# Scores and V of eight attention heads as eight float32 products in 64 x 32 tiles, with V taken from the float32 W1 in every batch

## Chip, cores and metric

One core of one Trainium2 chip. The metric is the device time of one execution in microseconds (us). TensorE (PE) does the matrix products, VectorE (DVE), ScalarE (ACT) and GpSimd (POOL) the elementwise work, SyncE (SP) issues the DMAs.

## What is computed

Inputs are float64. Attention between 512 positions and 32 state rows per head, 8 batches of 8 heads with 64 columns each, then two MLPs over 4608 rows:

```python
scores = scale * np.matmul(x, state.transpose(0, 1, 3, 2))   # x [8, 8, 512, 64], state [8, 8, 32, 64]
a = softmax(scores)
xread = np.matmul(a, state)
a2 = softmax(scale * np.matmul(state, x.transpose(0, 1, 3, 2)))
sread = np.matmul(a2, x)
x = rows of concatenate([xread, sread], axis=2)              # 4608 x 512
h = x @ w_in                                                 # 512 x 1024
solu = h * softmax(h); ln = layer_norm(solu) * g_ln
y = ln @ w_out                                               # 1024 x 512
y = y @ moe2_w_in; out = (y * sigmoid(1.702 * y)) @ moe2_w_out   # 2048 wide
```

`softmax` divides by the sum plus 1e-9. The kernel uses that xread @ w_in = a @ (state @ w_in): V = state @ w_in has only 32 rows per head.

## The kernel before

The program is written as steps (engine, cost, function, tiles read and written, a due time `key`) that `Plan.plan` (line 170) puts in an order per engine by a list schedule: among the steps that are ready it takes the one that its costs let start first, PE steps by key, others by due time. Constants such as `KF`, `LOOK`, `M2A`, `COLD` and `PAIR` steer it. SBUF tiles are slots of kinds ("s" 71 slots of 2 KB a partition, "t", "y", "d"), PSUM is eight banks of 128 x 512 float32 (`banks`, line 157). Products of full precision are three fp32r products of high and low parts (`mm3`, line 430, lines 431 to 433: hi x hi, lo x hi, hi x lo). `to_f32` (line 440) makes float32 of a float64 tile with two ACT, three DVE and one POOL instruction (line 460), `split` (line 463) the high and low part (line 467).

`attention(b)` (line 513) handles one batch. A tile `xT[j]` holds two heads, 2j and 2j+1, on 64 partitions each. The states of the heads stand in `S2`, two fixed tiles with zeros in the other head's half, so that `state_T` (line 557) gives a block-diagonal `stT`, two transposes of 128 x 128 per batch. `scores(g)` (line 574, products at line 580) multiplies it with `xT` for four heads: two products of 128 rows (half of them zeros) by 64 columns of the array and 512 moving columns in float32, one in each column half. Two such groups make a batch; the softmax over positions and over states follows, `e2_T` (line 624) transposes, `read_s` (line 635, products at line 642) makes sread as 32 small products of 128 rows by 32 columns.

V has two forms. Batches 0 and 1 use `state_w1` (line 673, products at line 680): four groups like the scores' per batch, with the float32 W1 tiles as moving operand, high part by ACT (line 684), low part by DVE (line 685) straight from PSUM. From batch `DIRECT = 2` on, `state_w1_both` (line 688) takes two batches at once: stT is split, W1 is split into `W1s` (line 1230), and eight `mm3` triples make V of two batches in halves that ACT copies to SBUF (line 720) and `split` cuts. In odd batches ("turned") the heads stand the other way round.

`mlp1` (line 755) multiplies the softmax A with V and does SoLU and layer norm, `z_T` (line 830) transposes, `mlp1_out` (line 849) multiplies with W2. The second MLP (`up`, line 1007, `down`, line 1097) is a seven-product scheme over 2 x 2 blocks, whose weights `prepare_up` (line 903) and `prepare_down` make and store in DRAM, and `load_up` (line 914) fetches once the first MLP's last product has run.

Of the kernel before, what the change touches and what calls it, by code (L numbers as in the profile page):

```python
# [25 lines left out]
KF = 11.222  # L26
LOOK = 27.436
KR = 1.553
DIRECT = 2
W1S = 20.477  # L30
ATT = -0.491
# [3 lines left out]
RK = 6  # L35
# [47 lines left out]
class Plan:  # L83
# [73 lines left out]
    def banks(self, kind, n):  # L157


        b = self.bank  # L160
        assert n == 1
        if kind == "w":
            if self.wide == 3:
# [3 lines left out]
        best = [(b[j] + (PAIR if b[j ^ 1] is not None else 0.0), b[j], (j,)) for j in range(8) if b[j] is not None]  # L167
        return min(best)[1:] if best else None
# [156 lines left out]
WAIT = 19.511  # L325
# [3 lines left out]
M1S = 14.290  # L329
M2A = 47.371  # L330
M2S = 3.016
A1 = 8.286
# [3 lines left out]
LD = 1.964  # L336
LA = 0.010
LOAD = dict(dve=LD, act=LA)
COLD = 16.0
IDLE = 2.2  # L340
XRAW = 1
BUS = 350e3

BUS0 = 180e3
BUS0T = 10.0
PAIR = 13.326
HOLDM = 1.958
HOLDW = 9.657
# [4 lines left out]
def attention_solu_gelu(ctx: ExitStack, tc: tile.TileContext, x, state, w1, w2, g_ln, w3, w4, out):  # L353
# [18 lines left out]
    SLOT = 40.411  # L372
# [14 lines left out]
    pl.kind("t", slot_p, 4)  # L387
# [36 lines left out]
    S2t = [pl.fixed(t, f"S2_{i}") for i, t in enumerate(S2)]  # L424
# [57 lines left out]
    A, V, xn, stT, W1s = {}, {}, {}, {}, {}  # L482
# [21 lines left out]
    def load_state(b):  # L504
        src = state[b].rearrange("(g h) n d -> h n g d", h=HG)

        def go(e):
            for hl in range(HG):
                e.dma_start(out=S2[b % 2][NS * hl:NS * hl + NS, :, hl % 2, :], in_=src[hl])

        do([(STQ, 3.)] if b == 0 else DMA(2.), go, writes=[S2t[b % 2]], nbytes=P * 512)

    def attention(b):
        base = (b - 1) * SLOT + (A1 if b == 1 else ATT)
        n_step = [0]
        steps = [16]

        def key():
            n_step[0] += 1
            return base + (n_step[0] - 1) * SLOT / steps[0]  # L520

        both = b >= DIRECT
        turned = both and b % 2
        xt = {}
        load_x(b, 0)
        if not turned:
            load_state(b)
# [29 lines left out]
        def state_T(c):  # L557
            p = tl("m", [P, 512], F32, f"pst{c}")
            s2 = S2t[c % 2]
            st = stT[c] = tl("t", [P, G, P], F32, f"stT{c}")  # L560

            def go(e):
                for g in range(G):
                    e.transpose(p()[:, g * P:(g + 1) * P], s2()[:, g].rearrange("p a d -> p (a d)"), ident)

            def v():
                return p()[:, 0:G * P].rearrange("p (g n) -> p g n", g=G)

            do(PE(.22), go, [s2], [p], key())
            do([("act", .27), ("dve", .33)], lambda e: copy(e, st(), v()), [p], [st])  # L570
# [3 lines left out]
        def scores(g):  # L574
            p = tl("m", [P, 512], F32, f"psc{b}_{g}")

            def go(e):
                for i in range(2):
                    jj = i ^ turned
                    e.matmul(p()[64 * i:64 * i + 64, :], stT[b]()[:, g, 64 * jj:64 * jj + 64], xt[2 * g + jj](),  # L580
                             start=True, stop=True)

            do(PE(.9), go, [stT[b], xt[2 * g], xt[2 * g + 1]], [p], key())
# [51 lines left out]
        def read_s():  # L635
            p = tl("m", [P, 512], F32, f"psr{b}")

            def go(e):
                for g in range(G):
                    for c in range(C):  # L640
                        for hl in range(HG):
                            e.matmul(p()[NS * hl:NS * hl + NS, g * D:(g + 1) * D],
                                     e2k[g]()[:, c, NS * hl:NS * hl + NS],
                                     xn[b, 2 * g + (hl // 2 ^ turned)]()[:, c, hl % 2, :],
                                     start=(c == 0), stop=(c == C - 1))

            do(PE(1.55), go, [e2k[0], e2k[1]] + [xn[b, j] for j in range(NP)], [p], key())
            sr = tl("t", [P, G, 2, D], F32, f"sr{b}")
            for g in range(G):
                do(DVE(.26), lambda e, g=g: e.tensor_scalar(  # L650
                    sr()[:, g], p()[:, g * D:(g + 1) * D].unsqueeze(1).to_broadcast([P, 2, D]),
                    r2[g]()[:, 1:2], None, op0=ALU.mult), [p, r2[g]], [sr])
            p2 = tl("m", [P, 512], F32, f"psrT{b}")

            def go2(e):
                for g in range(G):
                    e.transpose(p2()[:, g * P:(g + 1) * P], sr()[:, g].rearrange("p a d -> p (a d)"), ident)

            do(PE(.22), go2, [sr], [p2], key())
            for q in range(2):  # L660
                for a in range(2):
                    def go3(e, q=q, a=a):
                        pv = p2()[:, 0:G * P].rearrange("p (j a n) -> p j a n", a=2, n=NS)
                        o = xs[q]()[64 * a:64 * a + 64, :, b * NS:(b + 1) * NS]
                        if turned:
                            for j in range(2):
                                copy(e, o[:, j], pv[64 * a:64 * a + 64, 2 * q + 1 - j, a, :])
                        else:
                            copy(e, o, pv[64 * a:64 * a + 64, 2 * q:2 * q + 2, a, :])
                    c = 1 + bool(turned)  # L670
                    do([("act", .11 * c), ("dve", .13 * c)], go3, [p2], [xs[q]])

        def state_w1(g, f):
            p = tl("m", [P, 512], F32, f"pv{b}_{g}_{f}")
            hi = tl("s", [P, 512], F32R, f"vhi{b}_{g}_{f}")
            lo = tl("s", [P, 512], F32R, f"vlo{b}_{g}_{f}")

            def go(e):
                for jj in range(2):
                    e.matmul(p()[64 * jj:64 * jj + 64, :], stT[b]()[:, g, 64 * jj:64 * jj + 64],  # L680
                             W1[2 * g + jj, f](), start=True, stop=True)

            do(PE(.9), go, [stT[b], W1[2 * g, f], W1[2 * g + 1, f]], [p], key())
            do(ACT(.48), lambda e: e.copy(hi(), p()), [p], [hi])
            do(DVE(.6), lambda e: e.tensor_tensor(lo(), p(), hi(), op=ALU.subtract), [p, hi], [lo])
            V[b, g, f] = (hi, lo)

        def state_w1_both():


            hi = tl("s", [P, G, 4, 64], F32R, f"sthi{b}")
            lo = tl("s", [P, G, 4, 64], F32R, f"stlo{b}")
            for i in range(2):
                st = stT[b + i]

                def part(t, i=i):
                    return t()[:, :, 1:3, :] if i else t()[:, :, 0:4:3, :]

                def src(st=st):
                    return st().rearrange("p g (j n) -> p g j n", j=2)  # L700

                do([("act", .29), ("dve", .2)], lambda e, part=part, src=src: copy(e, part(hi), src()), [st], [hi])
                do([("pool", .68), ("dve", .33)], lambda e, part=part, src=src: e.tensor_tensor(
                    part(lo), src(), part(hi), op=ALU.subtract), [st, hi], [lo])
            for f in range(2):
                for g in range(G):
                    v = [tl("s", [P, 512], F32, f"v{b + i}_{g}_{f}") for i in range(2)]
                    for jj in range(2):
                        p = tl("m", [P, 512], F32, f"pv{b}_{g}_{f}_{jj}")

                        def go(e, p=p, g=g, f=f, jj=jj):
                            wh, wl = W1s[2 * g + jj, f]
                            at = [t()[:, g, 2 * jj:2 * jj + 2, :].rearrange("p i n -> p (i n)") for t in (hi, lo)]
                            mm3(p(), *at, wh(), wl(), True, True)

                        do(PE(.65), go, [hi, lo, *W1s[2 * g + jj, f]], [p], key())
                        for side in range(2):
                            t = v[side ^ jj]
                            r = slice(64 * side, 64 * side + 64)
                            do([("act", .48), ("dve", .6)], lambda e, t=t, p=p, r=r: copy(e, t()[r, :], p()[r, :]),  # L720
                               [p], [t])
                    for i in range(2):
                        V[b + i, g, f] = split(v[i], f"v{b + i}_{g}_{f}", None)
# [3 lines left out]
        if not turned:  # L727
            state_T(b)
        e0 = scores(0)
        x_T(2)  # L730
        x_T(3)
        e2_T(0, e0)
        e1 = scores(1)
        n_step[0] += 1
        if both and not turned:
# [583 lines left out]
```

## Time and profile before

| | |
|---|---|
| runs | 1121.33, 1122.02, 1122.55 us; median 1122.02 |
| profiled execution | span 1120.6 us from first to last instruction; no other time of it is given |
| busy, share of the span | PE 96%, DVE 72%, ACT 57%, POOL 26% |
| chain that ended last | PE 80%, DVE 6%, POOL 3%, ACT 3%, DMA issue 3% |
| PE clock by 40 slices | full in all but the first (9 tenths) and second (7 tenths) |

The span counts from the first instruction to the last; the runs are measured around it. A busy PE is not PE at its peak, since products are pipelined: the distance from one start to the next tells more than a duration. A float32 product shows as two records (passes), an fp32r product as one. A line can be a helper's (467, 472), then the tile tells what it is.

### The profile page before, as it was taken

Reading aid. Unit: us, or ns where it says so; the run is one execution under the profiler, and the core shown is the slowest. Engines: PE = TensorE matmul, PEld = TensorE weight load, DVE = VectorE, ACT = ScalarE, POOL = GpSimd, SP = SyncE. Lnnn points to the kernel's source line nnn. Section 1 sums busy time; section 2 is a strip of 40 time slices with the busy share of each in tenths; the row PEclk is TensorE's granted clock in tenths of the full one; section 3 lists DMA queues with packets and bytes.
Section 4 is the critical chain, followed back from the end, with each engine's and each line's share of the span. In section 5 each row is a group of like instructions: output and inputs, shape, how many; then the busy total and the mean of one; then the engine's idle time right before and its main releaser. Section 6 shows DMA issues by size and latency. Waiting matters only on the chain.

```text
span 1120.6 us, 21706 instructions
## 1 busy us (share of the span) xinstructions
PE 1080.8 (96%) x8055; PEld 977.5 (87%) x8055; DVE 802.0 (72%) x1372; ACT 639.9 (57%) x1172; POOL 286.6 (26%) x243
## 2 busy tenths in 40 slices
PE   5799999899889999999999999999999999999998
PEld 3367777677667889999999999999999999999998
DVE  7889768787887736638766755534398888788874
ACT  6588756866857547547656665545244444344341
POOL 3976653863756601401000000000000000000000
PEclk9799999999999999999999999999999999999999
DMA  8214243568663469999666757469944254344421
GB/s 238 72 58 104 69 94 97 173 135 199 178 148 94 151 158 369 343 344 314 233 236 230 245 192 261 170 224 398 389 127 131 66 171 143 105 141 151 139 88 58
DMA packets 233082, 202.78 MB, mean 181 GB/s; under 512 B 128784, under 2 KB 174864, under 8 KB 232976
## 3 DMA queue, kind: packets, MB, share of 16 engines
q1 hardware_dynamic: 232880, 201.26, 57.3%
q8 instruction: 63, 1.03, 0.4%
q14 instruction: 43, 0.35, 0.1%
q10 hardware_dynamic: 96, 0.13, 0.0%
HBM read 113.25 MB, written 82.84 MB: 175 GB/s over the span
## 4 chain that ended last, share of the span: by engine, by line
PE 80%; DVE 6%; POOL 3%; ACT 3%; SPq 3%; issue 3%; DMA 2%; DVEq 0%; POOLq 0%; ACTq 0%
PE psum L1107 9%; PE psum L1108 9%; PE psum L1109 9%; PE psum L1019 9%; PE psum L1020 9%; PE psum L1021 9%; PE psum L431 6%; PE psum L432 6%; PE psum L433 6%; SPq L815 2%; DVE sml L780 1%; PE psum L836 1%; DVE u L784 1%; DVE z L825 1%; POOL w_w L460 1%
## 5 line engine op out<-in xcount | busy, mean ns | idle before, releaser
L1107 PE MATMUL psum<-w4r,hi_g 128*128 128x256 f32 x896 | 251.7, 281 | 1.6 <-DVE oc L1118 1.6
L1109 PE MATMUL psum<-w4r,lo_g 128*128 128x256 f32 x896 | 251.5, 281 | 0.0
L1108 PE MATMUL psum<-w4r,hi_g 128*128 128x256 f32 x896 | 251.5, 281 | 0.0
L1107 PEld LDWEIGHTS psum<-w4r,hi_g 128*128 128x128 f32 x896 | 169.0, 189 | 1.8 <-ACT hi_g L472 1.8
L1109 PEld LDWEIGHTS psum<-w4r,lo_g 128*128 128x128 f32 x896 | 168.9, 189 | 0.0
L1108 PEld LDWEIGHTS psum<-w4r,hi_g 128*128 128x128 f32 x896 | 168.9, 188 | 0.0
L472 ACT CAST hi_g<-a_g 128x512 fp32r<-128x512 f32 x124 | 75.5, 621 | 128.1 <-DVE a_g L889 89.4
L460 POOL TENSOR_TENSOR w_w<-w_w,raw_w 128x512 uint32<-128x512 uint32 x48 | 66.5, 1390 | 270.0 <-DVE w_w L458 160.1
L431 PE MATMUL psum<-zhi,hi_w 128*128 128x512 f32 (+1 forms) x288 | 114.6, 398 | 6.0 <-DVE u L784 4.7
L1031 DVE TENSOR_TENSOR c<-psum,u 128x512 f32<-128x512 f32 x64 | 44.2, 690 | 93.2 <-PE psum L1021 63.9
L433 PE MATMUL psum<-zhi,lo_w 128*128 128x512 f32 (+1 forms) x288 | 110.4, 383 | 0.4 <-POOL lo_w L467 0.4
L966 DVE TENSOR_TENSOR lo_g<-a_g,hi_g 128x512 fp32r<-128x512 f32 x128 | 84.1, 687 | 20.6 <-PE psum L1108 7.4
L1003 ACT ACTIVATE t<-c 128x512 f32<-128x512 f32 x96 | 60.3, 632 | 40.6 <-DVE c L1031 40.5
L966 DVE TENSOR_TENSOR lo_g<-gr,hi_g 128x512 fp32r<-128x512 f32 x104 | 71.2, 687 | 11.9 <-ACT hi_g L472 9.2
L432 PE MATMUL psum<-zlo,hi_w 128*128 128x512 f32 (+1 forms) x208 | 78.6, 378 | 0.0
L472 ACT CAST hi_g<-gr 128x512 fp32r<-128x512 f32 x104 | 61.9, 619 | 28.8 <-PE psum L1108 15.3
L431 PEld LDWEIGHTS psum<-zhi,hi_w 128*128 128x128 f32 x288 | 54.6, 190 | 19.8 <-DVE u L784 6.4
L433 PEld LDWEIGHTS psum<-zhi,lo_w 128*128 128x128 f32 x288 | 54.5, 189 | 12.2 <-POOL lo_w L467 0.8
L1019 PE MATMUL psum<-hi_x,w3r_2h 128*128 128x256 f32 x224 | 63.0, 281 | 0.5 <-ACT x L1026 0.5
L1020 PE MATMUL psum<-lo_x,w3r_3h 128*128 128x256 f32 x224 | 63.0, 281 | 0.0
L1020 PE MATMUL psum<-lo_x,w3r_0h 128*128 128x256 f32 x224 | 63.0, 281 | 0.0
L1019 PE MATMUL psum<-hi_x,w3r_3h 128*128 128x256 f32 x224 | 62.9, 281 | 0.0
(252 smaller groups left out, 3109.2 us busy)
## 6 DMA issues: line engine op xcount, KB each, us to landing
g<-t SPq DMA_DIRECT2D x136, 256.0 KB, 3.4
gr<-g SPq DMA_DIRECT2D x136, 256.0 KB, 3.7
w4r<-w4k SPq DMA_DIRECT2D x56, 256.0 KB, 5.2
raw_w<-in_moe_w_in SPq DMA_DIRECT2D x24, 512.0 KB, 5.3
raw_w<-in_moe_w_out SPq DMA_DIRECT2D x24, 512.0 KB, 4.7
xb<-scr SPq DMA_DIRECT2D x34, 256.0 KB, 5.4
scr<-x SPq DMA_DIRECT2D x16, 512.0 KB, 3.9
out<-oc SPq DMA_DIRECT2D x32, 256.0 KB, 3.2
```

Source lines behind the costliest of these rows:

```text
L431: nc.tensor.matmul(o, lhi, rhi, start=first, stop=False)
L432: nc.tensor.matmul(o, lhi, rlo, start=False, stop=False)
L433: nc.tensor.matmul(o, llo, rhi, start=False, stop=last)
L460: do(POOL(1.23), lambda e: e.tensor_tensor(u(), u(), raw()[:, :, 0], op=ALU.add), [w, raw], [w], key=due)
L472: e.copy(o, i)
L966: do(DVE(.68), lambda e: e.tensor_tensor(flat_(lo), flat_(t), flat_(hi), op=ALU.subtract), [t, hi], [lo], key=due)
L1019: nc.tensor.matmul(o, wh()[:, k, cut], hi()[:, k, :], start=first and not mi + k, stop=False, **OPEN)
L1020: nc.tensor.matmul(o, wh()[:, k, cut], lo()[:, k, :], start=False, stop=False, **OPEN)
L1021: nc.tensor.matmul(o, wl()[:, k, cut], hi()[:, k, :], start=False, stop=bool(mi and k), **OPEN)
L1107: nc.tensor.matmul(o, hi()[:, mi, cut], wt[:, 0], start=first, stop=False, **OPEN)
L1108: nc.tensor.matmul(o, hi()[:, mi, cut], wt[:, 1], start=False, stop=False, **OPEN)
L1109: nc.tensor.matmul(o, lo()[:, mi, cut], wt[:, 0], start=False, stop=2 * j + mi == NM - 1 and u == 1, **OPEN)
```

## The change

The heads are grouped by parity: r = 0 the even heads, r = 1 the odd ones. `state_T` makes one transpose per batch, without zeros: partitions 64r to 64r+63 hold the heads of parity r, columns 32c to 32c+31 head 2c+r. A new function `by_heads` multiplies all eight heads in one step, each as a float32 product of 64 rows by 32 columns of the array, parity 0 into one PSUM bank and parity 1 into another. It serves the scores (one step per batch in place of two) and V (two steps per batch, every batch, in place of both old forms):

```diff
+        def by_heads(p, rhs):
 
             def go(e):
-                for g in range(G):
...
+                for c in range(HG):
+                    for r in range(2):
+                        e.matmul(p[r]()[NS * c:NS * c + NS, :], stT[b]()[D * r:D * r + D, NS * c:NS * c + NS],
+                                 rhs[c]()[D * r:D * r + D, :], start=True, stop=True)
+
+            do(PE(HEADS), go, [stT[b], *rhs], p, key())
...
+        def state_w1(f):
+            p = [tl("m", [P, 512], F32, f"pv{b}_{r}_{f}") for r in range(2)]
+            by_heads(p, [W1[c, f] for c in range(HG)])
+            for r in range(2):
...
+                do(ACT(.48), lambda e, hi=hi, r=r: e.copy(hi(), p[r]()), [p[r]], [hi])
+                do(DVE(.6), lambda e, hi=hi, lo=lo, r=r: e.tensor_tensor(lo(), p[r](), hi(), op=ALU.subtract),
+                   [p[r], hi], [lo])
+                V[b, r, f] = (hi, lo)
...
-        if not turned:
-            state_T(b)
-        e0 = scores(0)
+        state_T()
         x_T(2)
         x_T(3)
...
+        p = [tl("m", [P, 512], F32, f"psc{b}_{r}") for r in range(2)]
+        by_heads(p, [xt[c] for c in range(HG)])
+        e2 = [soft(r, p[r]) for r in range(2)]
...
-        if b + 1 == DIRECT:
+        if b + 1 < B:
+            attention(b + 1)
+        if b + 1 == B:
             for f in range(2):
                 for k in range(KD):
-                    W1s[k, f] = split(W1[k, f], f"w1s_{k}_{f}", b * SLOT + W1S + 2 * (k + KD * f))
-        if b + 1 < B:
-            attention(b + 1)
+                    W1s[k, f] = split(W1[k, f], f"w1s_{k}_{f}", b * SLOT - 10 + k + KD * f)
```

`soft` is the old softmax without the product. `S2`, its two memsets, `turned` and `state_w1_both` are gone; the split W1 is used for the 256 state rows' `mlp1` alone, and W1 in float32 stays until the last V. The state output needs one transpose in place of two. `banks` can give two banks at once, "t" has 8 slots in place of 4, `RK` (buffers kept free for `load_up`) is 8 in place of 6, and some twenty of the planner's constants are new (`KF` 11.222 to 10.181, `WAIT` 19.511 to 43.673, `HEADS` 1.060, ...), so that the order of the whole program is made anew.

On PE, around V of batch 2 (names: `hi_w1s_k_f` and `w_w1_k_f` tile k, f of W1, `sthi2` and `stlo2` the split states of batches 2 and 3, `zhi0`, `u1` of the MLP of batches 0 and 1), before:

```order
L431 MATMUL psum_69<-hi_w1s_0_0_497,sthi2_913 128x512
L432 MATMUL psum_69<-lo_w1s_0_0_507,sthi2_913 128x512
L433 MATMUL psum_69<-hi_w1s_0_0_497,stlo2_958 128x512
L836 MATMUL psum_69<-ident_79,u0_0_696 128x128
L836 MATMUL psum_69<-ident_79,u0_1_736 128x128
L836 MATMUL psum_69<-ident_79,u0_2_761 128x128
L836 MATMUL psum_69<-ident_79,u0_3_847 128x128
L431 MATMUL psum_69<-zhi0_5_1073,hi_w2_5_1145 128x512
L432 MATMUL psum_69<-zlo0_5_1087,hi_w2_5_1145 128x512
L433 MATMUL psum_69<-zhi0_5_1073,lo_w2_5_1157 128x512
L431 MATMUL psum_69<-hi_w1s_1_0_517,sthi2_913 128x512
```

and now:

```order
L566 MATMUL psum_69<-w_w1_0_1_414,stT2_941 32x512 x2
L566 MATMUL psum_69<-w_w1_1_1_450,stT2_941 32x512 x2
L566 MATMUL psum_69<-w_w1_2_1_458,stT2_941 32x512 x2
L566 MATMUL psum_69<-w_w1_3_1_508,stT2_941 32x512 x2
L558 MATMUL psum_69<-ident_79,st3_1140 128x128
L566 MATMUL psum_69<-xT3_0_1299,stT3_1429 32x512 x2
L566 MATMUL psum_69<-xT3_1_1343,stT3_1429 32x512 x2
L566 MATMUL psum_69<-xT3_2_1359,stT3_1429 32x512 x2
L566 MATMUL psum_69<-xT3_3_1377,stT3_1429 32x512 x2
L766 MATMUL psum_69<-ident_79,u1_0_937 128x128
L766 MATMUL psum_69<-ident_79,u1_1_969 128x128
L766 MATMUL psum_69<-ident_79,u1_2_1078 128x128
```

The triples that stood between products of the first MLP's output have become two groups of eight; behind the second, the transpose of state 3 and the scores of batch 3 follow at once, then four transposes and A x V of batch 2.

On POOL, in the start (`w_w1_k_f` and `lo_w1s_k_f` a tile of W1 and its low part, `s1` softmax of batch 0, `alo` the low part of A), before:

```order
L460 TENSOR_TENSOR w_w1_0_1_442<-w_w1_0_1_442,raw_w1_0_1_316 128x512
L460 TENSOR_TENSOR w_w1_1_1_449<-w_w1_1_1_449,raw_w1_1_1_324 128x512
L467 TENSOR_TENSOR lo_w1s_2_0_553<-w_w1_2_0_380,hi_w1s_2_0_522 128x512
L467 TENSOR_TENSOR lo_w1s_3_0_560<-w_w1_3_0_389,hi_w1s_3_0_542 128x512
L467 TENSOR_TENSOR lo_w1s_0_1_567<-w_w1_0_1_442,hi_w1s_0_1_551 128x512
L467 TENSOR_TENSOR lo_w1s_1_1_574<-w_w1_1_1_449,hi_w1s_1_1_558 128x512
L612 TENSOR_TENSOR s1_0_1_383<-s1_0_1_383,z1_0_1_569 128x512
L460 TENSOR_TENSOR w_w1_2_1_470<-w_w1_2_1_470,raw_w1_2_1_326 128x512
L460 TENSOR_TENSOR w_w1_3_1_512<-w_w1_3_1_512,raw_w1_3_1_444 128x512
L619 TENSOR_TENSOR alo0_0_596<-aT0_0_581,ahi0_0_585 128x512
L619 TENSOR_TENSOR alo0_1_610<-aT0_1_583,ahi0_1_590 128x512
```

and now:

```order
L467 TENSOR_TENSOR lo_w1s_3_0_553<-w_w1_3_0_386,hi_w1s_3_0_541 128x512
L460 TENSOR_TENSOR w_w1_0_1_414<-w_w1_0_1_414,raw_w1_0_1_312 128x512
L460 TENSOR_TENSOR w_w1_1_1_450<-w_w1_1_1_450,raw_w1_1_1_316 128x512
L460 TENSOR_TENSOR w_w1_2_1_458<-w_w1_2_1_458,raw_w1_2_1_320 128x512
L460 TENSOR_TENSOR w_w1_3_1_508<-w_w1_3_1_508,raw_w1_3_1_372 128x512
L602 TENSOR_TENSOR s1_0_0_375<-s1_0_0_375,z1_0_0_566 128x512
L602 TENSOR_TENSOR s1_0_1_384<-s1_0_1_384,z1_0_1_571 128x512
L467 TENSOR_TENSOR lo_w1s_0_1_598<-w_w1_0_1_414,hi_w1s_0_1_560 128x512
L609 TENSOR_TENSOR alo0_0_610<-aT0_0_595,ahi0_0_602 128x512
L609 TENSOR_TENSOR alo0_1_622<-aT0_1_604,ahi0_1_615 128x512
```

The four tiles of W1's second half (line 460) now follow each other; four low parts of W1 and a softmax multiplication (line 612, now 602) stood between them. Both softmax multiplications of batch 0 now come behind the last tile, and the low parts of A behind those.

## Rows read from the trace of the kernel before

**Rows 1.** Three stretches: length, busy PE, PEld, DVE, ACT, POOL (count), clock, DMA share, GB/s

```profile
0.00:46.55 46.55, 27.87 (x150) 11.48 (x150) 35.44 (x61) 27.91 (x55) 29.64 (x28) 0.83 0.65 187
46.55:420.00 373.45, 358.18 (x2050) 272.75 (x2050) 291.07 (x537) 259.43 (x497) 218.01 (x189) 0.99 0.49 124
420.00:1120.60 700.60, 694.76 (x5859) 693.22 (x5857) 475.53 (x775) 352.54 (x620) 38.91 (x27) 1.00 0.62 211
```

**Rows 2.** PE's four longest waits by line, 46.6 to 420 us: us, times, longest

```profile
PE psum L431 <- DVE u L784: 6.2, 7, 2.8
PE psum L630 <- ACT e2t L592: 1.7, 1, 1.7
PE psum L657 <- DVE sr L650: 1.7, 2, 1.0
PE psum L836 <- POOL u L795: 1.4, 2, 1.1
```

**Rows 3.** Timeline of PE in the start: start, us, line, count, [idle before]

```profile
27.16 1.84 PE L580 MATMUL psum<-xT,stT 128*64 128x512 f32 x4 [3.55 <-ACT stT L472]
...
43.40 3.22 PE L680 MATMUL psum<-w_w,stT 128*64 128x512 f32 x4 [5.04 <-POOL w_w L460]
46.55 0.80 PE L431 MATMUL psum<-vhi,ahi 128*128 128x512 f32 x1
```

**Rows 4.** Timeline of POOL in the start

```profile
21.81 3.37 POOL L605 TENSOR_TENSOR s<-s,m 128x512 f32<-128x512 f32 x1 [2.15 <-DVE m L604]
...
35.23 5.86 POOL L467 TENSOR_TENSOR lo_w1s<-w_w,hi_w1s 128x512 fp32r<-128x512 f32 x4
41.06 1.04 POOL L612 TENSOR_TENSOR s<-s,z 128x512 f32<-128x512 f32 x1
...
44.55 2.51 POOL L619 TENSOR_TENSOR alo<-aT,ahi 128x512 fp32r<-128x512 f32 x2
```

**Rows 5.** Timeline of PE around a score group of batch 4

```profile
185.97 0.39 PE L432 MATMUL psum<-zlo,hi_w 128*128 128x512 f32 x1
186.20 0.40 PE L433 MATMUL psum<-zhi,lo_w 128*128 128x512 f32 x1
186.53 1.08 PE L580 MATMUL psum<-xT,stT 128*64 128x512 f32 x4
187.54 0.66 PE L836 MATMUL psum<-ident,u 128*128 128x128 f32 x4
```

**Rows 6.** Timeline of PE around a read group

```profile
203.37 1.10 PE L642 MATMUL psum<-xn,e2k 128*32 128x64 f32 x64
204.48 0.65 PE L836 MATMUL psum<-ident,u 128*128 128x128 f32 x4
```

**Rows 7.** Timeline of PE, a state's two transposes

```profile
190.82 0.38 PE L564 MATMUL psum<-ident,S 128*128 128x128 f32 x2
191.04 0.60 PE L836 MATMUL psum<-ident,u 128*128 128x128 f32 x4
```

**Rows 8.** Timeline of SP's DMA issues in the start

```profile
17.21 2.27 SPq L1213 DMA_DIRECT2D g_sb<-in_moe_g_ln  x1
...
21.87 0.37 SPq L445 DMA_DIRECT2D raw_w<-in_moe_w_in  x1
```

**Rows 9.** Groups by line and shape, 0 to 420 us: count, busy us, mean ns

```profile
L467 POOL TENSOR_TENSOR lo_v<-v,hi_v 128x512 fp32r<-128x512 f32 x23 | 30.5, 1331 | 1.5 <-issue 1.0 <-DVE hi_v L474 0.4
L472 ACT COPY v<-psum 64x512 f32<-64x512 f32 x48 | 27.5, 581 | 2.7 <-PE psum L433 2.0
L472 ACT CAST hi_v<-v 128x512 fp32r<-128x512 f32 x18 | 11.0, 616 | 0.1
L685 DVE TENSOR_TENSOR vlo<-psum,vhi 128x512 fp32r<-128x512 f32 x8 | 5.3, 680 | 1.1 <-ACT vhi L684 1.1
L684 ACT CAST vhi<-psum 128x512 fp32r<-128x512 f32 x8 | 4.7, 584 | 3.4 <-PE psum L680 3.3
```

More of the change, by code (lines that the diff above doesn't have):

```diff
@@ L25 @@
 AHEAD = 30.092
[L26 to L29, printed above, removed]
+KF = 10.181
+LOOK = 27.681
+KR = 0.745
+STEPS = 13.000
+LATEV = 99
+HEADS = 1.060
 W1S = 20.477
-ATT = -0.491
+ATT = -0.468
 ZL = 7.738
@@ L166, in banks @@
             return min(best) if best else None
-        best = [(b[j] + (PAIR if b[j ^ 1] is not None else 0.0), b[j], (j,)) for j in range(8) if b[j] is not None]
-        return min(best)[1:] if best else None
+        best = sorted((b[j] + (PAIR if b[j ^ 1] is not None else 0.0), b[j], j) for j in range(8) if b[j] is not None)
+        if len(best) < n:
+            return None
+        return max(t for _, t, _ in best[:n]), tuple(j for *_, j in best[:n])
     def plan(self):
@@ L328 @@
 M1A = -3.168
[L329 to L332, printed above, removed]
+M1S = 14.618
+M2A = 48.714
+M2S = 3.142
+A1 = 4.656
 DMAQ = 0
@@ L335 @@
 WARM = 7
-LD = 1.964
-LA = 0.010
+LD = 1.875
+LA = -0.409
 LOAD = dict(dve=LD, act=LA)
-COLD = 16.0
-IDLE = 2.2
+COLD = 18.042
+IDLE = 2.200
 XRAW = 1
[L342 to L348, printed above, removed]
+BUS = 347350.590
+BUS0 = 170067.709
+BUS0T = 8.428
+PAIR = 14.200
+HOLDM = 2.261
+HOLDW = 9.169
 HOLD = dict(m=HOLDM, w=HOLDW)
@@ L504, in load_state @@
     def load_state(b):
-        src = state[b].rearrange("(g h) n d -> h n g d", h=HG)
+        t = st_raw[b] = tl("t", [P, 2, D], F32, f"st{b}")
+        src = state[b].rearrange("(c r) n d -> c n r d", r=2)
         def go(e):
-            for hl in range(HG):
-                e.dma_start(out=S2[b % 2][NS * hl:NS * hl + NS, :, hl % 2, :], in_=src[hl])
-        do([(STQ, 3.)] if b == 0 else DMA(2.), go, writes=[S2t[b % 2]], nbytes=P * 512)
+            for c in range(HG):
+                e.dma_start(out=t()[NS * c:NS * c + NS], in_=src[c])
+        do([(STQ, 3.)] if b == 0 else DMA(2.), go, writes=[t], nbytes=P * 512)
     def attention(b):
@@ L638, in go @@
             def go(e):
-                for g in range(G):
+                for g in range(2):
                     for c in range(C):
@@ L653, in read_s @@
+            for g in range(2):
+                do(DVE(.2), lambda e, g=g: e.tensor_scalar(sr()[:, g], p()[:, g * D:(g + 1) * D], r2[g]()[:, 1:2], None,
+                                                           op0=ALU.mult), [p, r2[g]], [sr])
             p2 = tl("m", [P, 512], F32, f"psrT{b}")
[L655 to L659, printed above, removed]
+            do(PE(.12), lambda e: e.transpose(p2()[:, 0:P], sr().rearrange("p r d -> p (r d)"), ident), [sr], [p2], key())
@@ L660, in read_s @@
             for q in range(2):
[L661 to L723, printed above, removed]
@@ L725, in attention @@
         x_T(0)
         x_T(1)
-        if not turned:
-            state_T(b)
-        e0 = scores(0)
+        state_T()
         x_T(2)
         x_T(3)
[L732 to L735, printed above, removed]
-            load_state(b + 1)
-            state_T(b + 1)
-        e2_T(1, e1)
-        read_s()
-        if both and not turned:
-            n_step[0] -= 1
-            steps[0] = VST
-            state_w1_both()
-        if not both:
-            for f in range(2):
-                for g in range(G):
-                    state_w1(g, f)
+        p = [tl("m", [P, 512], F32, f"psc{b}_{r}") for r in range(2)]
```

70 lines of the change are left out of this document (32 added, 38 removed).

## Prediction

> **What bounds the kernel now.** I read the table by stretches first. The span of 1120.6 us falls into three [rows 1]. Up to 46.55 us TensorE (PE) is busy for only 27.87 us, at a granted clock of 0.83 of full. From there to 420 us, the rest of attention and the first MLP, it is busy for 358.18 of 373.45 us at 0.99. After 420 us, in the second MLP, it is busy for 694.76 of 700.60 us. The change touches nothing that the third stretch computes, so its time must show in the first two.
>
> The list of PE's waits in the second stretch comes next. PE is idle there for 15.3 us in all (373.45 - 358.18), and VectorE (DVE) ends 7.9 us of the four longest waits (6.2 + 1.7) [rows 2]. So there PE's own instructions set the pace, with other engines close behind (DVE 291.07, ACT 259.43 of 373.45 us). A microsecond taken from PE there is a microsecond of the end, as far as nobody else becomes late.
>
> The first stretch is another matter. PE sits idle 5.04 us for a W1 tile from GpSimd (POOL) just ahead of the last V group of batch 0 at 43.40, and the first full product starts at 46.55 [rows 3]. POOL itself works without a pause from 21.81 to 47 us [rows 4]. PE instructions saved there are worth nothing; a POOL queue that ends sooner is worth something.
>
> **The price of a group of small products.** A score group today is two float32 products in the two column halves of the array, two passes each, four records. It starts at 186.53 and the next work at 187.54: 1.01 us. The product ahead started at 186.20, 0.33 before it, where full products follow each other at 0.23: 0.10 for the way in [rows 5]. So 1.11 us. The two halves do run side by side: one product alone would need two passes of about 0.5, and two in turn 2.0.
>
> The group that reads the state goes further: 32 products, 64 records of 64 columns. At 0.5 x 64/512 = 0.063 each they would take 4.0 us in turn; they take 1.11, from 203.37 to 204.48 [rows 6]. Four column quarters, each with its own moving operand over 128 rows, run at once.
>
> The new group has the same two passes of 512 columns, on four column quarters times two row halves. The columns are covered by [rows 6]; no row shows two row halves at once. Bounds: 1.01, as today's group; 2.02, if the row halves take turns; 8.1 with all eight in turn. I take 1.06 and 0.10 for the way in, 1.16: the value next to the read group, where sixty records beyond the first four add about 0.10 over 16 x 0.063, so that 0.05 for twelve more is ample. The ends stay for the rivals.
>
> **The sum on PE.** Removed: 16 score groups and 8 V groups of batches 0 and 1 at 1.11 = 26.6; 24 V triples of batches 2 to 7 in full-array products, at three times 0.23 = 0.69 [rows 5], 16.6; 32 state transposes at (191.04 - 190.82)/2 = 0.11 [rows 7], 3.5. Together 46.7. Added: 24 groups at 1.16 = 27.8 and 16 transposes, 1.8; together 29.6. PE has 17.1 us less to do. Of this, 8 groups and 6 transposes (9.5) become 4 groups and 3 transposes (5.0) ahead of the first full product, where PE waits anyway. **What counts is 17.1 - 4.5 = 12.6 us.**
>
> **The start.** Up to the second low part of A, the order gives POOL one W1 low part fewer, 5.86/4 = 1.47 us [rows 4]. The last W1 tile, loaded at 21.87 behind g (17.21) and a state load [rows 8], is issued ahead of both: 4.7 us of queue. Against it, both softmax multiplications of batch 0 (1.04 us) now stand behind that tile, and A behind them. Bounds: 6 us sooner (both gains) and 2 us later (the two multiplications, unhidden). I take 3 us sooner, between the two gains.
>
> **What becomes later.** A V eviction used to be two copies of half a bank, a cast and a POOL subtraction; now it is an ACT cast and a DVE subtraction straight from PSUM. For batches 2 to 7 ACT loses 48 x 0.581 + 18 x 0.616 = 39.0 and gains 24 x 0.584 = 14.0; POOL loses 23 x 1.331 = 30.6; DVE gains 24 x 0.680 = 16.3 [rows 9]. DVE thus rises from 291 to about 307 of some 360 us. Four evictions of one batch take DVE 2.7 us, and in batch 2 only a transpose, a score group and four transposes, 0.11 + 1.16 + 0.44 = 1.7 us of PE work, stand between the second V group and A x V. Behind a product that waits there, everything else on PE waits too. Bounds: 2 us for each of six batches (12) and, since POOL and ACT are relieved, 5 us of today's 15.3 gone. Scaling DVE's 7.9 by 16/291 gives 0.4; with some added waits at the V groups I take 1.5. The transpose of state 3 now stands right ahead of its score group, so PE waits for the copy: 3.55 us where ACT's queue was full [rows 3], nothing where the copy is hidden; I take 1.
>
> The Trainium skill, page TensorEngine Tiling (Array Packing), section PSUM Bottleneck, speaks against the change: tiling speeds up TensorE but not the emptying of PSUM, which may then bind. By that rule alone the 12 us of the upper bound would be taken and the sum would be some 10 us worse.
>
> Free of cost: the planner's new constants, because they act only through the order, which is counted here; the state loads, 32 DMAs before and after; W1's split, which POOL and ACT still take in the start though its key is now late. W1 itself stays to the last V, 8 buffers more than before, but the V of one batch at a time needs 8 fewer than the V of two. Were they short, loads for the second MLP would slip; its first stretch shows no PE idle time that tells how near that is.
>
> **Sum**: -12.6 - 3 + 1.5 + 1 = -13.1. The profiled execution's span is 1120.6, the median of the runs 1122.02, 1.4 above it. 1120.6 - 13.1 + 1.4 = **1109 us**.
>
> **Rivals.** (a) *The row halves take turns* and the change does not do what its form says. A group is then 2.02 + 0.10; the 20 groups outside the start cost 0.96 more, 19.2 us: 1128, slower. It decides from about 1.7 us a group on. For it: no row shows two row halves at work. Against it: four column quarters with 128 rows each already run at once [rows 6], and the two halves write two different banks. The Trainium skill names, on TensorEngine Tiling (Array Packing), section Tiling Modes, 64 x 32 as eight independent tiles; under Restrictions and Gotchas it says that row tiles cannot use one bank at the same time, which the two banks avoid. No row here shows either. (b) *Evictions eat the gain*: V arrives late in each batch, 12 us instead of 1.5: 1119.5. For it: DVE ends most of today's waits [rows 2]. Against: POOL and ACT get 30 and 25 us lighter. (c) *The start gives all it can and the waits shrink*: 3 us and 6.5 us better: 1099.5. For it: ACT and POOL end 3.1 us of [rows 2]; against: the start's long chain has POOL in it either way.
>
> **How the numbers follow.** Forecast 0.67, (a) 0.09, (b) 0.12, (c) 0.12. The range reaches from (c) to (b), 1098 to 1119, and leaves out (a) and the far tails, together under 0.2. A measurement can tell about 0.2%, 2.2 us. Faster: forecast and (c) nearly whole and two thirds of (b), 0.86. Same: 0.05. Slower: 0.09, that is (a).
>
> **What would show it.** A score or V group, eight products in 16 records, with about 1.06 us to the next start: right; 2.0: (a). First full product between 41 and 45 us. The copies of V gone from ACT. The second MLP starting 10 to 16 us sooner with the 700 us behind it unchanged; if that part grows, loads have slipped and the sum is wrong there. PE's waits on V's low parts (line 657 of the new kernel) at 1 to 3 us in all: forecast; over 8: (b).

## The result, and the profile after

The changed kernel takes **1111.31 us** (median of 4 runs, 1110.78 to 1113.23) against 1122.13 for the kernel before (4 runs, 1121.33 to 1122.55): a ratio of **0.9907, 95% interval 0.9893 to 0.9921**. The forecast was 1109, range 1098 to 1119. The profiled execution spans 1110.04 us, 10.5 less than before, at a granted clock of 0.988.

The table by stretches of the changed kernel, cut at the first full product and at the same work as 420 us before (columns as in [rows 1]):

```profile
0.00:44.89 44.89, 25.86 (x178) 10.79 (x178) 33.00 (x58) 25.52 (x50) 24.43 (x23) 0.85 0.68 192
44.89:410.50 365.61, 348.97 (x2220) 260.83 (x2221) 294.73 (x542) 235.05 (x442) 184.37 (x162) 0.99 0.50 127
410.50:1110.04 699.54, 695.81 (x5859) 694.77 (x5857) 480.81 (x775) 355.62 (x620) 39.46 (x27) 1.00 0.62 211
```

Against [rows 1] the start is 1.66 us shorter, the middle 7.84 and the rest about 1.0. In the middle PE is busy for 9.21 us less (358.18 to 348.97) and idle for 1.37 us more (16.64 against 15.27).

PE's timeline around a V group of batch 2 and the scores of batch 3 shows the price of the new form (columns as in [rows 3]):

```profile
115.12 0.40 PE L433 MATMUL psum<-zhi,lo_w 128*128 128x512 f32 x1
115.45 1.09 PE L566 MATMUL psum<-w_w,stT 64*32 64x512 f32 x16
116.47 0.33 PE L558 MATMUL psum<-ident,st 128*128 128x128 f32 x1
117.28 1.09 PE L566 MATMUL psum<-xT,stT 64*32 64x512 f32 x16 [0.47 <-ACT vhi L656]
118.30 0.66 PE L766 MATMUL psum<-ident,u 128*128 128x128 f32 x4
```

A group starts 0.33 us behind the product ahead (115.12 to 115.45; full products follow each other at 0.23) and the next work 1.02 us later: eight small products in 16 records take as long as two large ones in four [rows 5], where the forecast had 1.06. The row halves do run side by side: rival (a), with the halves in turn, has 2.02 us. The wait for state 3, put at 1 us in the forecast, is 0.47 (the row puts it down to the cast `vhi`; VectorE's copy of state 3 had ended only 0.15 us before the scores).

PE's waits up to 430 us, by line:

```profile
PE psum L620 <- ACT e2t L582: 7.2, 1, 7.2
PE psum L566 <- POOL w_w L460: 5.2, 4, 4.5
PE psum L431 <- DVE u L714: 4.7, 7, 2.2
PE psum L566 <- ACT stT L472: 2.4, 2, 1.4
...
PE psum L431 <- ACT ahi L472: 2.3, 1, 2.3
...
PE psum L431 <- DVE vlo L657: 0.9, 1, 0.9
```

V's low parts (`vlo`) are not among the longest. Of the two waits for a state's transpose (`stT`), the one of 1.4 us is in the middle. These rows of PE up to 430 us (count, busy us, mean ns, idle time before them and what ended it) are of the kernel before:

```profile
L431 PE MATMUL psum<-hi_v,ahi 128*128 128x512 f32 x96 | 39.5, 412 | 0.9 <-DVE u L784 0.9
L432 PE MATMUL psum<-lo_v,ahi 128*128 128x512 f32 x96 | 37.8, 394 | 0.0
L433 PE MATMUL psum<-hi_v,alo 128*128 128x512 f32 x96 | 37.8, 394 | 0.0
...
L431 PE MATMUL psum<-vhi,ahi 128*128 128x512 f32 x32 | 13.5, 422 | 0.7 <-DVE u L784 0.7
L432 PE MATMUL psum<-vlo,ahi 128*128 128x512 f32 x32 | 12.8, 400 | 0.0
L433 PE MATMUL psum<-vhi,alo 128*128 128x512 f32 x32 | 12.7, 397 | 0.0
```

and these of the changed one:

```profile
L431 PE MATMUL psum<-vhi,ahi 128*128 128x512 f32 x128 | 53.7, 420 | 6.3 <-DVE u L714 2.9 <-ACT ahi L472 2.3 <-DVE vlo L657 0.9
L433 PE MATMUL psum<-vhi,alo 128*128 128x512 f32 x128 | 51.9, 406 | 1.2 <-POOL alo L609 1.2
L432 PE MATMUL psum<-vlo,ahi 128*128 128x512 f32 x128 | 51.8, 405 | 0.0
```

PE itself waits 0.9 us for V's low parts (its weight loads another 1.5). But the same 384 products of A x V, which the change does not touch, take 157.4 us in place of 154.1. These are busy times of records that overlap; from start to start, without idle time, it is 95.8 in place of 92.5. The clock tells why. Between the first full product and the second MLP the changed kernel has three stretches in which TensorE was granted half its clock, 1.2 of 2.4 GHz (below them the 50 us behind the first full product; columns as above):

```profile
46.70:50.10 3.40, 3.40 (x10) 2.62 (x9) 2.99 (x9) 2.12 (x6) 3.27 (x4) 0.50 0.00 0
63.80:67.20 3.40, 3.40 (x16) 2.01 (x22) 2.06 (x5) 2.57 (x8) 2.26 (x2) 0.50 0.05 19
299.30:302.70 3.40, 3.40 (x9) 2.63 (x8) 2.58 (x5) 0.00 (x0) 3.23 (x3) 0.50 0.80 214
44.89:95.00 50.11, 44.17 (x290) 31.60 (x290) 45.86 (x88) 41.24 (x83) 36.52 (x30) 0.93 0.16 53
```

The kernel before has less of it there, the end of a stretch of the start and one more:

```profile
46.55:47.80 1.25, 1.25 (x4) 1.06 (x4) 0.75 (x2) 0.59 (x1) 1.25 (x2) 0.50 0.00 0
320.90:324.30 3.40, 3.40 (x8) 2.72 (x9) 2.15 (x7) 1.63 (x5) 1.05 (x1) 0.50 0.65 97
```

That is 10.2 us at half clock against 4.7. If each of these microseconds is counted as half lost, A x V takes 92.0 and 91.9 us: what it grew by is the clock. Over all products of the middle the loss is 2.8 us larger than before, half of the difference, so of the PE time that the change saves, 2.8 us is handed back in these two executions. This was not in the forecast at all. Ahead of the first stretch PE had been idle for 2.27 us waiting for A of batch 0 and for 0.62 us for its low part; ahead of the second for 2.21 us, up to 62.26, for VectorE; ahead of the third for 0.89 us for a low part of V and for 0.61 us for one of A.

That the change as such costs clock is not shown. The mean granted clock of a whole execution (its start included) is 0.989 over the nine executions of the changed kernel and 0.989 over 35 of the kernel before.

### The profile page after: what moved, and what is told of

Read it like the earlier page. It is cut to its first block, busy times and chain, and to the rows that moved or that the text cites. A ratio compares the mean times of both kernels' runs of the same rounds, so it can differ in the third digit from the quotient of the medians.

```text
span 1110.0 us, 22067 instructions
## 1 busy us (share of the span) xinstructions
PE 1070.6 (96%) x8255; PEld 966.4 (87%) x8255; DVE 808.5 (73%) x1374; ACT 616.2 (56%) x1111; POOL 248.3 (22%) x212
## 3 DMA queue, kind: packets, MB, share of 16 engines
q8 instruction: 65, 1.06, 0.4%
## 4 chain that ended last, share of the span: by engine, by line
PE 79%; DVE 6%; SPq 4%; POOL 4%; DMA 2%; issue 2%; ACT 2%; POOLq 0%; DVEq 0%; ACTq 0%
PE psum L1039 10%; PE psum L1037 10%; PE psum L950 10%; PE psum L1038 10%; PE psum L951 10%; PE psum L949 10%; PE psum L431 5%; PE psum L433 5%; PE psum L432 5%; DMA raw_w<-in_moe_w_in 2%; POOL lo_w3s L467 2%; SPq L745 1%; PE psum L766 1%; PE psum L566 1%; DVE w_w L458 1%
## 5 line engine op out<-in xcount | busy, mean ns | idle before, releaser
L472 ACT CAST hi_g<-a_g 128x512 fp32r<-128x512 f32 x128 | 77.9, 620 | 108.5 <-DVE a_g L819 54.6
L961 DVE TENSOR_TENSOR c<-psum,u 128x512 f32<-128x512 f32 x64 | 44.1, 690 | 92.5 <-PE psum L951 57.3
L933 ACT ACTIVATE t<-c 128x512 f32<-128x512 f32 x96 | 60.5, 632 | 46.6 <-DVE c L961 43.0
L950 PE MATMUL psum<-lo_x,w3r_2h 128*128 128x256 f32 x224 | 63.0, 281 | 0.0
L951 PE MATMUL psum<-hi_x,w3r_3l 128*128 128x256 f32 x224 | 63.0, 281 | 0.0
L951 PE MATMUL psum<-hi_x,w3r_0l 128*128 128x256 f32 x224 | 62.9, 281 | 0.0
```

What stands on the lines that cost most here:

```text
L472: e.copy(o, i)
L950: nc.tensor.matmul(o, wh()[:, k, cut], lo()[:, k, :], start=False, stop=False, **OPEN)
L951: nc.tensor.matmul(o, wl()[:, k, cut], hi()[:, k, :], start=False, stop=bool(mi and k), **OPEN)
```

## The experiments

All compute the same outputs; e3, e4, e5, e8, e10, e11 and e12 do some of the work more than once. Times are medians, ratios are against the kernel before beside them. "First" is the start of the first full product; the middle runs from there to the first product of the second MLP, "idle" is PE's in it; "A x V" is the busy time of the three groups of products as above; "half clock" is the time in the middle at which TensorE was granted half its clock. The last five columns are of one profiled execution each.

| kernel | time, us | ratio, 95% interval | first | middle | idle | A x V | half clock |
|---|---|---|---|---|---|---|---|
| before | 1122.1 | | 46.55 | 389.76 | 15.27 | 154.1 | 4.7 |
| changed | 1111.3 | 0.9907 (0.9893 to 0.9921) | 44.89 | 381.92 | 16.64 | 157.4 | 10.2 |
| e1 new form, old constants | 1115.6 | 0.9942 (0.9928 to 0.9957) | 40.54 | 387.05 | 23.20 | 153.9 | 13.7 |
| e2 old form, new constants | 1121.5 | 0.9994 (0.9984 to 1.0005) | 46.32 | 393.05 | 16.07 | 156.0 | 12.5 |
| e3 V products twice | 1117.8 | 0.9957 (0.9940 to 0.9973) | 43.99 | 390.93 | 17.12 | 154.9 | 3.4 |
| e4 V's low parts twice | 1125.3 | 1.0028 (1.0018 to 1.0039) | 45.55 | 394.71 | 26.19 | 159.3 | 13.7 |
| e5 V twice, batches 0 and 1 | 1109.1 | 0.9886 (0.9872 to 0.9899) | 44.16 | 381.50 | 15.78 | 156.9 | 10.2 |
| e6 W1's split late (batch 4) | 1106.4 | 0.9857 (0.9840 to 0.9873) | 39.36 | 383.95 | 18.97 | 158.4 | 9.8 |
| e7 W1's split late (batch 0) | 1110.6 | 0.9901 (0.9885 to 0.9916) | 39.68 | 385.61 | 18.82 | 157.2 | 13.7 |
| e8 e5 and e6 together | 1104.5 | 0.9845 (0.9832 to 0.9859) | 39.41 | 380.29 | 17.64 | 153.5 | 0 |
| e9 changed, again | 1111.8 | 0.9905 (0.9890 to 0.9921) | 44.77 | 380.30 | 15.29 | 157.0 | 10.2 |
| e10 one wait filled | 1111.1 | 0.9898 (0.9884 to 0.9911) | 43.06 | 382.74 | 17.50 | 157.1 | 10.2 |
| e11 e6 with one wait filled | 1106.7 | 0.9853 (0.9837 to 0.9868) | 39.05 | 384.38 | 20.56 | 155.1 | 6.8 |
| e12 e8 again | 1104.6 | 0.9840 (0.9827 to 0.9853) | 39.84 | 380.97 | 17.22 | 155.4 | 3.4 |

With each microsecond at half clock counted as half, A x V takes 91.5 to 92.6 us from start to start in all of these profiles but that of e1 (93.6). So its differences below are differences of the clock.

**e1 and e2: form or constants?** The change carries new planner constants besides the new form. e1 keeps the form and puts the old constants back, e2 the reverse:

```diff
-KF = 10.181
+KF = 11.222
...
-WAIT = 43.673
+WAIT = 19.511
```

> The new form of scores and V, with the planner's constants of the kernel before (HEADS, STEPS and LATEV, which only the new form has, stay). Theory A: the gain is TensorE's own time, 8 products side by side in 1.02 us in place of 1.01 us for two; then most of the gain is kept, 1110 to 1117 us. Rival R: the gain comes from the new constants and the order that they make; then 1119 us or more.

> The kernel before, with the new values of the twenty constants that both kernels have. Theory A: 1119 to 1126 us, no gain. Rival R: 1111 to 1116 us.

The form alone gives 6.5 us (1122.1 to 1115.6), the constants alone nothing that can be measured (0.9994), and together 10.8. So the form is the cause of the first 6.5 us, and the constants are worth 4.3 us only on top of it: with the old ones the first full product comes 4.4 us sooner (40.54), but PE is idle for 23.20 us in the middle, with the new ones for 16.64. Of the 23.20 us, 5.5 are rival (b) of the prediction, PE waiting for V's evictions on VectorE; the longest of these waits in e1:

```profile
PE psum L566 <- DVE vlo L657: 2.2, 1, 2.2
PE psum L632 <- DVE vlo L657: 1.9, 1, 1.9
PE psum L558 <- DVE vlo L657: 1.2, 1, 1.2
```

The forecast had counted the constants as free.

**e3: is a microsecond of PE a microsecond of the end?** Every V group issues its products twice, so PE gets back what the V part of the change had saved:

```diff
-            do(PE(HEADS), go, [stT[b], *rhs], p, key())
+            def twice(e):
+                go(e)
+                if rhs[0] is W1.get((0, 0)) or rhs[0] is W1.get((0, 1)):
+                    go(e)
+
+            do(PE(HEADS), twice, [stT[b], *rhs], p, key())
```

> The changed kernel with the eight products of each of the 16 V groups issued twice over the same banks, everything else in the same order. Theory A, TensorE sets the pace behind the start: 14 groups there cost some 0.95 us more each, +11 to +14 us, 1122 to 1126 us. Rival S, other engines set the pace and TensorE has slack: under +6 us, below 1118 us.

The time rises by 6.5 us in the medians, half of what Theory A expected and a little over what Rival S allowed; between the two profiled executions it is 8.1 us. The V groups do take 12.0 us more in the middle (start to start, without idle time), so the price of the products is right. But 6.8 us less is spent at half clock, which is 3.4 us of work; PE is idle for 0.5 us more, and the first full product comes 0.9 sooner. These add up to the 8.1 us but for 0.1. The half clock at 46.7 and 63.8 us is gone, and of the later ones a single stretch is left, at 235.4 us:

```profile
43.99:94.00 50.01, 42.71 (x322) 30.12 (x322) 45.51 (x87) 41.48 (x82) 36.55 (x30) 1.00 0.17 54
```

Read so, a microsecond of PE is a microsecond of the end, and the part that does not show came back through the clock. The four executions of e3 have a mean granted clock of 0.992, against 0.989 of the changed kernel.

**e4: how much room has VectorE?** V's low parts are computed twice, 32 more instructions of 0.675 us, 21.6 us of VectorE:

```diff
...
+                    for _ in range(2):
+                        e.tensor_tensor(lo(), p[r](), hi(), op=ALU.subtract)
...
```

> The changed kernel with VectorE's subtraction that makes V's low part done twice, 32 times 0.67 us more on VectorE, everything else in the same order. Theory A: VectorE has slack, +1 to +7 us, 1112 to 1118 us. Rival S, VectorE's emptying of PSUM sets the pace: +15 to +21 us, 1126 to 1132 us.

14.0 us slower, twice the most that the forecast's theory allowed and near its rival. PE's idle time in the middle rises by 9.6 us, and the longest wait is now the one that the rival (b) of the prediction names. PE's waits up to 430 us in e4:

```profile
PE psum L431 <- DVE vlo L659: 8.2, 5, 3.0
PE psum L620 <- ACT e2t L582: 6.4, 1, 6.4
```

So VectorE stands right beside the path: 0.65 us of the end for each microsecond that it gets there. Part of that is clock: e4 spends 3.4 us more at half clock, which is 1.7 of the 14.0 us. The scaling of the forecast (DVE's waits times 16/291) was far too mild as a rule. It did little harm here, where VectorE got little more to do (see below). e4 lengthens V's low parts and fills VectorE's queue at once; which of the two costs more it does not tell.

**e5, e9, e10: what the clock has to do with it.** e5 doubles V's products for batches 0 and 1 alone; e9 is the changed kernel once more, for a second profile; e10 issues only the second V group of batch 0, right ahead of A x V, three times:

```diff
+                if b < 2 and (rhs[0] is W1.get((0, 0)) or rhs[0] is W1.get((0, 1))):
+                    go(e)
...
+                if b == 0 and rhs[0] is W1.get((0, 1)):
+                    go(e)
+                    go(e)
```

> The changed kernel with the eight V products of each half issued twice for batches 0 and 1 alone (four more groups, two of them ahead of the first full product); the order and the result are the same. Theory C (part of the gain was lost because TensorE is granted half its clock in two stretches of 3.4 us at 46.7 and 63.8 us, which follow idle time of TensorE in the start): the doubled groups keep it at work there, A x V takes 92.2 to 93.8 us as in the run with all V products doubled instead of 95.8, two groups outside the start add 1.9 us, and the time is 1108.5 to 1111.5, no longer than the changed kernel. Rival N (the clock has nothing to do with it; doubled groups cost what they take): A x V stays at 95.8, the first full product comes up to 2 us later, and the time is 1113 to 1115.5.

> The changed kernel itself, once more, for a second profile of the same instructions. Theory C (the half clock at 46.7 and 63.8 us follows from idle time of TensorE that the order of this kernel makes, so it comes back in every execution): TensorE is again at half its clock somewhere from 44.9 to 70 us, A x V takes 95 to 96.6 us, time 1110 to 1113. Rival R (where it falls changes from one execution to the next, and one profile tells little): A x V between 92 and 97, with another pattern.

> The changed kernel with one group alone issued three times: the second V group of batch 0, which stands right ahead of the first full product, where TensorE now idles for 2.27 us. The two extra issues take about 1.9 us of that idle time; nothing else is moved and the result is the same. Theory C: the first full product stays at 44.5 to 45.2 us, TensorE is at its full clock right behind it, A x V takes 92.5 to 94.5 us, and the time is 1108 to 1110, 1.5 to 3.3 below the changed kernel's run beside it. Rival N (the filled idle time has no bearing on the clock): A x V 95 to 96.6, time within 1 us of the changed kernel.

e9 shows the half clock again from 46.93 us, as in the first profile, but the later stretches at 81.06 and 231.26, not at 63.8 and 299.3; the sum is again 10.2 us and A x V 157.0. The loss repeats, its later places move. e10 fills the wait, PE idles only 0.45 us, and the clock right behind it is full; the first full product, at 43.06 us, comes 1.5 us sooner than Theory C had it. PE's timeline of the changed kernel, where the records grow from 0.40 to 0.63 us as the clock falls:

```profile
41.57 1.05 PE L566 MATMUL psum<-w_w,stT 64*32 64x512 f32 x4 [0.19 <-POOL w_w L460]
44.89 0.50 PE L431 MATMUL psum<-vhi,ahi 128*128 128x512 f32 x1 [2.27 <-ACT ahi L472]
45.23 0.40 PE L432 MATMUL psum<-vlo,ahi 128*128 128x512 f32 x1
46.25 0.50 PE L433 MATMUL psum<-vhi,alo 128*128 128x512 f32 x1 [0.62 <-POOL alo L609]
46.59 0.51 PE L431 MATMUL psum<-vhi,ahi 128*128 128x512 f32 x1
46.90 0.63 PE L432 MATMUL psum<-vlo,ahi 128*128 128x512 f32 x1
```

and of e10:

```profile
35.11 7.50 PE L566 MATMUL psum<-w_w,stT 64*32 64x512 f32 x48 [4.46 <-POOL w_w L460]
43.06 0.50 PE L431 MATMUL psum<-vhi,ahi 128*128 128x512 f32 x1 [0.45 <-ACT ahi L472]
...
46.71 0.40 PE L433 MATMUL psum<-vhi,alo 128*128 128x512 f32 x1
46.95 0.39 PE L431 MATMUL psum<-vhi,ahi 128*128 128x512 f32 x1
```

Yet A x V takes 157.1 us in e10: half clock comes at 60.48 instead, the three stretches of the middle again sum to 10.2 us, and the time, 1111.1, is within 1 us of the changed kernel's, as Rival N has it. Theory C holds for the place and fails for the sum. e5 is faster than the changed kernel by 2.2 us in the median (2.7 against e9), with intervals that still overlap a little, and A x V falls only to 156.9, which misses Theory C's bound of 93.8 us start to start (it is 95.3); Rival N's 1113 to 1115.5 is missed as well, and Theory C's 1108.5 to 1111.5 is met. The profiled execution of e5 is its slowest, with a clock of 0.987 where the other three have 0.991 to 0.994, so how much clock e5 saves is not shown by its profile. Filling one wait moves the half clock; in e10 it does not save it.

**e6 and e7: what sets the start.** The split of W1, which only the 256 state rows' part of the first MLP needs, is planned into GpSimd's queue in the start. The timeline of GpSimd in the changed kernel:

```profile
26.19 2.43 POOL L595 TENSOR_TENSOR s<-s,m 128x512 f32<-128x512 f32 x2
28.59 5.69 POOL L467 TENSOR_TENSOR lo_w1s<-w_w,hi_w1s 128x512 fp32r<-128x512 f32 x4
35.24 6.28 POOL L460 TENSOR_TENSOR w_w<-w_w,raw_w 128x512 uint32<-128x512 uint32 x4 [0.96 <-DMA st<-in_state]
41.47 2.05 POOL L602 TENSOR_TENSOR s<-s,z 128x512 f32<-128x512 f32 x2
43.48 1.27 POOL L467 TENSOR_TENSOR lo_w1s<-w_w,hi_w1s 128x512 fp32r<-128x512 f32 x1
```

W1's last four conversions (35.24) stand behind four low parts (28.59) that nobody needs yet, and the softmax's multiplications (41.47), which A waits for, stand behind both. In the kernel before, W1's last conversions come later, but with a multiplication ahead of them [rows 4]:

```profile
42.06 2.53 POOL L460 TENSOR_TENSOR w_w<-w_w,raw_w 128x512 uint32<-128x512 uint32 x2
```

e6 makes the casts of W1's split wait for the first MLP of batch 4, e7 for that of batch 0:

```diff
...
-                    W1s[k, f] = split(W1[k, f], f"w1s_{k}_{f}", b * SLOT - 10 + k + KD * f)
+                    W1s[k, f] = split(W1[k, f], f"w1s_{k}_{f}", b * SLOT - 10 + k + KD * f, after=[last[4]])
```

> The changed kernel with the split of W1 for the first MLP held back until the first MLP of batch 4 has been placed, so that GpSimd and ScalarE make none of its parts in the start; the rest of the order is planned anew. Theory P (the start is set by the softmax and A behind GpSimd's queue, in which five of W1's low parts of about 1.4 us stand): the first full product moves from 44.9 to 38 to 41.5 us, and the time is 1104 to 1109. Rival Q (the start is set by the loads and by VectorE's own chain, GpSimd is only beside it): the first full product stays at 43.5 to 45.5 and the time within 2 us of 1111, or later by 2 to 5 us if the parts then come late in the middle.

> As the run before, but W1's split waits only for the first MLP of batch 0. Theory P: the same start, 38 to 41.5 us to the first full product, and 1104 to 1109; Rival Q: first full product at 43.5 to 45.5, time 1109 to 1116. If this and the run before differ by over 3 us with the same start, the place of the split in the middle is what the rest hangs on.

With the split, its low parts on GpSimd and its casts on ScalarE are gone from the start in e6, the rest is planned anew, and the multiplications come at 35.95:

```profile
29.74 6.24 POOL L460 TENSOR_TENSOR w_w<-w_w,raw_w 128x512 uint32<-128x512 uint32 x4 [2.36 <-ACT xT L472]
35.95 2.05 POOL L602 TENSOR_TENSOR s<-s,z 128x512 f32<-128x512 f32 x2
39.38 1.29 POOL L609 TENSOR_TENSOR alo<-aT,ahi 128x512 fp32r<-128x512 f32 x1 [1.39 <-ACT ahi L472]
```

The first full product comes 5.5 us sooner (39.36) and the time is 1106.4, 4.9 less, as Theory P had it: the middle grows by 2.0, and the second MLP takes 1.0 less. e7 has the same start (39.68) and is 4.2 us slower than e6, outside the 1104 to 1109 of Theory P; of the 3.3 us between their profiled spans 1.7 lie in the middle and 1.3 behind it. The place of the split matters by more than the 3 us that the expectation set as its mark. e7 spends 13.7 us of the middle at half clock and e6 9.8, which is 1.9 us of work and covers the part in the middle; what the part behind it comes from stays open.

**e8, e11 and e12: both, and the best.**

> Both edits: W1's split held back to batch 4 and the V products of batches 0 and 1 issued twice. Theory C with P: A x V at 92.2 to 93.8 us and the first full product at 38.5 to 42, 1102 to 1108, no slower than the split held back alone. Rival N: 2 to 4 us slower than the split held back alone, by what the doubled groups take.

> W1's split held back to batch 4, and only the second V group of batch 0 issued three times. Theory C: no half clock right behind the first full product at 39.3 to 39.8 us, A x V 92.5 to 94.5 us instead of 96.6, time 1103 to 1105.5. Rival N: A x V at 95.5 to 97, time 1105.5 to 1108.

> The fastest kernel so far (W1's split held back to batch 4, the V products of batches 0 and 1 issued twice) once more, beside the others of this call. Theory C: A x V again at 92.2 to 93.8 us, full clock from 39.4 to 410 us, time 1103.5 to 1106. Rival R: half clock in other places, A x V 94 to 97.

e8 and e12 are one kernel measured twice: 1104.5 and 1104.6 us, the fastest here, about 7 us below the changed kernel (its interval of the ratio, 0.9832 to 0.9859, lies wholly below 0.9893). Against e6 it does 1.3 us more of V on PE in the middle and is 1.9 us faster, though the two intervals overlap. In e8's profile the clock is full from 39.41 to 410 us:

```profile
39.41:89.50 50.09, 43.83 (x340) 30.18 (x340) 46.67 (x89) 43.05 (x85) 33.09 (x28) 1.00 0.17 56
80.00:410.00 330.00, 317.33 (x2012) 238.69 (x2011) 260.32 (x476) 205.71 (x383) 164.29 (x143) 1.00 0.56 142
```

A x V takes 153.5 us there and 155.4 in e12, where a stretch at 274 us is at half clock: Theory C's bound of 93.8 us start to start holds in e8 (92.6) and is missed by 0.4 in e12. e11, which fills only the one wait, brings A x V to 155.1 as expected (94.1 start to start) but no time: PE's idle time in the middle rises by 1.6, and 1106.7 is e6's. What decides how many half-clock stretches an execution gets stays open: e8 and e12 (153.5 and 155.4) against e6 (158.4) say that the doubled groups help, not by which of them. All executions point the same way: the granted clock is 0.991 to 0.998 in the nine of e8 and e12, 0.994 in the mean, and 0.990 to 0.992 in the four of e6.

## Why the prediction came out

The time fell in the range, 2.3 us above the forecast. By its steps, on the spans (10.5 where 13.1 was forecast):

- **PE's work: right.** Start to start and without idle time, scores fell by 6.06 us in the middle, V by 4.94, and the two kinds of state transposes by 1.44: 12.4 for a forecast of 12.6. The choice of 1.06 between bounds of 1.01 and 2.02 was confirmed at 1.02. Rival (a), row halves in turn, falls.
- **The start: right in sign, half in size.** 1.66 us for 3. W1's last conversion did end 3.1 us sooner, at 41.5 us in place of 44.6. But the multiplications behind the last W1 tile held A back: PE waits 2.27 us for A at 44.89. e6 shows what the forecast left aside, since both kernels have it: W1's split in the start costs 5.5 us, in a kernel where it is not needed until batch 7.
- **The waits: right in size, by luck.** 1.4 us more idle time for a forecast of 2.5 (V's evictions 1.5, the state 1). V's low parts take 0.9 and two copies of a state 1.9; the other waits became shorter, those on VectorE's `u` 4.7 us for the 6.2 of [rows 2]. VectorE was to rise to about 307 us; it is busy for 294.73. The forecast had counted only ACT's and POOL's share of V's old casts and subtractions; VectorE had done six of the casts (3.1 us) and a subtraction (1.6) itself, and was also rid of three casts of A (1.6) and some small copies. Twenty multiplications (line 755, before 825) also took 975 ns each in place of 1116, 2.8 us less. With the load that the forecast assumed, e4's rate gives an estimate of (307 - 294.7) x 0.65 = 8 us more, not far from rival (b), and with the old constants (e1) PE did wait 5.5 us for V's evictions. That (b) stayed away hung on a lighter VectorE and on an order that the forecast had not worked out.
- **ACT and POOL: right.** ACT falls by 24.4 us in the middle (25.0 forecast), POOL by 33.6 (30.6). V's copies on ACT are gone.
- **The constants as free: wrong.** The step said that they act only through the order, which was counted. They do, but the count looked at places, not at the 6.6 us of idle time between e1 and the changed kernel, nor at the start, where e1's order is 4.4 us better.
- **PE's unchanged work as unchanged: wrong.** This is the step that takes most of the difference: A x V 3.3 us longer at a lower granted clock, 2.8 over all products of the middle. It holds for the two profiled executions; between the kernels' mean clocks no difference is shown.
- **Behind 420 us: almost as said.** About 1.0 us shorter, where no change was forecast; loads did not slip. Of the marks that the prediction set, the second MLP's start is missed by a little (436.31 to 426.81, 9.5 us sooner for 10 to 16) and PE's wait for V's low parts (0.9 for 1 to 3); the group (1.02) and the first full product (44.89, in 41 to 45) are met.

The sum of the misses: 0.2 (PE) + 1.3 (start) - 1.1 (waits) + 3.2 (work left as it was, by the clock above all) - 1.0 (the rest) = 2.6, the difference between 13.1 and 10.5. Misses of 4.7 and 2.1 us cancel in part, so the nearness of the number is in part luck; the price of the products, which carries the forecast, is not. The Trainium skill (TensorEngine Tiling (Array Packing), section PSUM Bottleneck) says that tiling speeds up TensorE but not the emptying of PSUM. The forecast put its price at some 10 us, an estimate; here PE waited 0.9 us for V's low parts. It waited 8.2 us for them in e4, where VectorE's part of the emptying was made 21.6 us longer, and 5.5 us for V's evictions in e1.

## What to carry to other kernels

Where two small products fill only part of the array, put as many into one group as there are free tiles: here the time of a group followed its columns and passes, not its products. Before counting a saving on a busy engine as time, look for what becomes idle, or late, right behind it; here VectorE had almost no slack, and in the two profiled executions 2.8 of the 12.4 us of PE time saved went back to a lower granted clock. Read the clock of several executions before you put that down to a change: a single profile of each kernel cannot tell it from the spread between executions. And read the queue ahead of the instruction that the first stage waits for: the largest gain of a single edit found afterwards (e6) was to move work out of it that nobody needed for another 300 us.

## What was not expected of the hardware

- Eight float32 products of 64 x 32 with 512 columns, in 16 records and two banks, take 1.02 us, as two of 128 x 64 do, plus 0.10 on the way in.
- Adding work to TensorE made other work on it shorter: with the V products doubled (e3), 12.0 us more of them cost 6.5 us in time (8.1 between the profiled executions), and A x V fell from 157.4 to 154.9 us, with 3.4 us at half clock in place of 10.2.
- The same kernel has half-clock stretches in places that repeat (46.7 and 46.9 us) and in places that move (63.8 and 299.3 us, 81.1 and 231.3 us) between two executions with the same instructions, 10.2 us in both.
- Half clock came also where PE had been idle for only 0.89 and 0.61 us shortly before (at 299.3 us in the changed kernel).
